# Sparse attention and a hardswish FFN as one pipeline over 384-token tiles, with head pairs on 128 partitions

## The chip, the cores and the metric

One core of a Trainium2 chip. The metric is the device time of one execution in microseconds (us). Engines: PE (matrix multiply; PEld its weight loads), DVE (vector), ACT (scalar), POOL (GpSimd), SP (issues DMA only). "Clock" is the share of full speed that the throttle granted the PE.

## The reference

Inputs q, k, v are (4 batches, 8 heads, 768 tokens, 64), float32. Cut to what matters:

```python
k_sum = k.reshape(B, H, 24, 32, D).max(axis=3)       # one summary per block of 32 keys
v_sum = v.reshape(B, H, 24, 32, D).mean(axis=3)
mask  = |i - j| < 16                                 # local window
scores = concat(where(mask, q k^T / 8, -1e9), q k_sum^T / 8 + log(32))
x = softmax(scores) @ concat(v, v_sum)               # to (3072 tokens, 512)
h = x @ w_in                                         # 512 -> 2048
out = (h * clip(h + 3, 0, 6) / 6) @ w_out            # 2048 -> 512
```

## The kernel before

A Tile scheduler orders its instructions. Heads go one by one; tokens sit in blocks of 128:

```python
for b in range(B):
    for h in range(H):
        ...  # qs, ks, vsf: float32 loads through SP, two buffers each
        for st in range(ST):                              # 6 blocks of 128 tokens
            tp = ps.tile([64, 128], F32, tag="scr")
            nc.tensor.transpose(tp[:], qs[:, st, :], ident[:])
            nc.vector.tensor_copy(qT[:, st * 128:(st + 1) * 128], tp[:])
            ...  # the same for ks; later six of v with reduce_sum
        for jt in range(ST):
            nc.tensor.matmul(sp[:, :w], klhs, qr, start=True, stop=True)     # up to 128 x 384
            nc.vector.tensor_scalar_mul(ap[:, :w], sp[:, :w], scl)
            nc.gpsimd.affine_select(out=ap[:, :w], ...)   # two of them: the band
            nc.scalar.activation(ap[:, :w], ap[:, :w], AF.Exp)
        ...
        for st in range(ST):
            ...  # up to 4 matmuls into op [128, 65], reciprocal, scale, transpose, copy
            nc.sync.dma_start(out=x4[b, h, :, st * 128:(st + 1) * 128], in_=oT[:])   # to a DRAM scratch
...
for tt in range(TT):                                      # 6 tiles of 512 tokens, x read back
    for ft in range(NFT):
        ...  # FFN1: 4 matmuls into hp [128, 512]
        nc.vector.tensor_scalar(hs[:], hp[:], 3.0, 0.0, op0=ALU.add, op1=ALU.max)
        nc.vector.tensor_scalar(gt, hs[:], 6.0, 1.0 / 6.0, op0=ALU.min, op1=ALU.mult)
        nc.vector.tensor_tensor(gt, gt, hp[:], op=ALU.mult)
    ...  # FFN2: per 128 tokens 16 matmuls into [128, 512], copy, store
```

The softmax here doesn't subtract the row's maximum and nothing guards it: scores larger than these inputs give would overflow.

Of the kernel before, what the change touches and what calls it, by code (L numbers as in the profile page):

```python
# [9 lines left out]
F32 = mybir.dt.float32  # L10
BF16 = mybir.dt.bfloat16
AF = mybir.ActivationFunctionType
ALU = mybir.AluOpType
AX = mybir.AxisListType


@with_exitstack
def kernel(
# [9 lines left out]
    nc = tc.nc  # L28
    B, H, S, D = q.shape
    block, window = 32, 16  # L30
    nb = S // block
    scl = 1.0 / math.sqrt(D)
    logb = math.log(block)
    NEG = -1.0e9
    ST = S // 128
    d_model = H * D
    n_tok = B * S
    d_ff = moe_w_in.shape[1]

    x_dram = nc.dram_tensor("x_scratch", (d_model, n_tok), BF16, kind="Internal").ap()  # L40
    x4 = x_dram.rearrange("(h d) (b s) -> b h d s", b=B, h=H)

    qv = q.rearrange("b h (st p) d -> b h p st d", p=128)
    kv = k.rearrange("b h (st p) d -> b h p st d", p=128)
    vv = v.rearrange("b h (st p) d -> b h p st d", p=128)

    sb = ctx.enter_context(tc.tile_pool(name="sb", bufs=2))
    ps = ctx.enter_context(tc.tile_pool(name="ps", bufs=2, space=bass.MemoryType.PSUM))
    const = ctx.enter_context(tc.tile_pool(name="const", bufs=1))

    ident = const.tile([128, 128], F32, tag="id")
    make_identity(nc, ident[:])
    identb = const.tile([128, 128], BF16, tag="idb")
    nc.vector.tensor_copy(identb[:], ident[:])
    ones = const.tile([128, 1], F32, tag="ones")
    nc.vector.memset(ones[:], 1.0)

    for b in range(B):
        for h in range(H):
            qs = sb.tile([128, ST, 64], F32, tag="qs")  # L60
            ks = sb.tile([128, ST, 64], F32, tag="ks")
            vsf = sb.tile([128, ST, 64], F32, tag="vsf")
            nc.sync.dma_start(out=qs[:], in_=qv[b, h])
            nc.sync.dma_start(out=ks[:], in_=kv[b, h])
            nc.sync.dma_start(out=vsf[:], in_=vv[b, h])
            vs = sb.tile([128, ST, 65], BF16, tag="vs")
            nc.vector.tensor_copy(vs[:, :, :64], vsf[:])
            nc.vector.memset(vs[:, :, 64:65], 1.0)
            qT = sb.tile([64, ST * 128], BF16, tag="qT")
            kT = sb.tile([64, ST * 128], BF16, tag="kT")  # L70
            for st in range(ST):
                tp = ps.tile([64, 128], F32, tag="scr")
                nc.tensor.transpose(tp[:], qs[:, st, :], ident[:])  # L73
                nc.vector.tensor_copy(qT[:, st * 128:(st + 1) * 128], tp[:])  # L74
                tp2 = ps.tile([64, 128], F32, tag="scr")
                nc.tensor.transpose(tp2[:], ks[:, st, :], ident[:])  # L76
                nc.vector.tensor_copy(kT[:, st * 128:(st + 1) * 128], tp2[:])  # L77
            ksT = sb.tile([64, nb], BF16, tag="ksT")
            nc.vector.reduce_max(ksT[:], kT[:].rearrange("d (n b) -> d n b", b=block), axis=AX.X)
            vsumT = sb.tile([64, nb], F32, tag="vsumT")  # L80
            for st in range(ST):
                tp = ps.tile([64, 128], F32, tag="scr")
                nc.tensor.transpose(tp[:], vsf[:, st, :], ident[:])  # L83
                nc.vector.reduce_sum(vsumT[:, st * 4:st * 4 + 4],  # L84
                                     tp[:].rearrange("d (n b) -> d n b", b=block), axis=AX.X)
            vsum = sb.tile([128, 65], BF16, tag="vsum")
            nc.vector.memset(vsum[:], 0.0)
            nc.vector.memset(vsum[:nb, 64:65], 1.0)  # L88
            vp = ps.tile([nb, 64], F32, tag="scr")
            nc.tensor.matmul(vp[:], vsumT[:], ident[:64, :64], start=True, stop=True)  # L90
            nc.vector.tensor_scalar_mul(vsum[:nb, :64], vp[:], 1.0 / block)

            ap_store = {}
            for jt in range(ST):
                st_lo = max(0, jt - 1)
                st_hi = min(ST, jt + 2)
                w = (st_hi - st_lo) * 128
                klhs = kT[:, jt * 128:(jt + 1) * 128]
                qr = qT[:, st_lo * 128:st_hi * 128]
                sp = ps.tile([128, 384], F32, tag="scr")  # L100
                nc.tensor.matmul(sp[:, :w], klhs, qr, start=True, stop=True)  # L101
                ap = sb.tile([128, 384], BF16, tag=f"ap{jt}")
                nc.vector.tensor_scalar_mul(ap[:, :w], sp[:, :w], scl)  # L103
                base = (jt - st_lo) * 128
                nc.gpsimd.affine_select(  # L105
                    out=ap[:, :w], in_=ap[:, :w], compare_op=ALU.is_ge, fill=NEG,
                    base=base + (window - 1), channel_multiplier=1, pattern=[[-1, w]])
                nc.gpsimd.affine_select(  # L108
                    out=ap[:, :w], in_=ap[:, :w], compare_op=ALU.is_ge, fill=NEG,
                    base=-base + (window - 1), channel_multiplier=-1, pattern=[[1, w]])  # L110
                nc.scalar.activation(ap[:, :w], ap[:, :w], AF.Exp)  # L111
                ap_store[jt] = (ap, st_lo)
            spA = sb.tile([nb, S], BF16, tag="spA")
            for half in range(2):
                sp = ps.tile([nb, 384], F32, tag="scr2")
                nc.tensor.matmul(sp[:], ksT[:], qT[:, half * 384:(half + 1) * 384],
                                 start=True, stop=True)
                nc.vector.tensor_scalar(spA[:, half * 384:(half + 1) * 384], sp[:], scl, logb,  # L118
                                        op0=ALU.mult, op1=ALU.add)
            nc.scalar.activation(spA[:], spA[:], AF.Exp)  # L120

            for st in range(ST):
                jts = [jt for jt in (st - 1, st, st + 1) if 0 <= jt < ST]
                nj = len(jts) + 1
                op = ps.tile([128, 65], F32, tag="op")
                for ii, jt in enumerate(jts):
                    ap, st_lo = ap_store[jt]
                    lhs = ap[:, (st - st_lo) * 128:(st - st_lo + 1) * 128]
                    nc.tensor.matmul(op[:], lhs, vs[:, jt, :], start=(ii == 0), stop=False)  # L129
                nc.tensor.matmul(op[:], spA[:, st * 128:(st + 1) * 128], vsum[:nb, :],  # L130
                                 start=False, stop=True)
                inv = sb.tile([128, 1], F32, tag="inv")
                nc.vector.reciprocal(inv[:], op[:, 64:65])
                o = sb.tile([128, 64], F32, tag="o")
                nc.vector.tensor_scalar_mul(o[:], op[:, :64], inv[:])  # L135
                otp = ps.tile([64, 128], F32, tag="scr")
                nc.tensor.transpose(otp[:], o[:], ident[:])  # L137
                oT = sb.tile([64, 128], BF16, tag="oT")
                nc.vector.tensor_copy(oT[:], otp[:])  # L139
                nc.sync.dma_start(out=x4[b, h, :, st * 128:(st + 1) * 128], in_=oT[:])  # L140

    KT = d_model // 128
    NFT = d_ff // 128
    MT = d_model // 128
    N_TOK_TILE = 512
    TT = n_tok // N_TOK_TILE

    wconst = ctx.enter_context(tc.tile_pool(name="wc", bufs=1))
    w_in_f = wconst.tile([128, KT, d_ff], F32, tag="winf")
    nc.sync.dma_start(out=w_in_f[:], in_=moe_w_in.rearrange("(kt p) f -> p kt f", p=128))  # L150
    w_out_f = wconst.tile([128, NFT, d_model], F32, tag="woutf")
    nc.sync.dma_start(out=w_out_f[:], in_=moe_w_out.rearrange("(ft p) dm -> p ft dm", p=128))
    w_in_sb = wconst.tile([128, KT, d_ff], BF16, tag="win")
    nc.vector.tensor_copy(w_in_sb[:], w_in_f[:])
    w_out_sb = wconst.tile([128, NFT, d_model], BF16, tag="wout")
    nc.vector.tensor_copy(w_out_sb[:], w_out_f[:])

    sb2 = ctx.enter_context(tc.tile_pool(name="sb2", bufs=2))
    ps2 = ctx.enter_context(tc.tile_pool(name="ps2", bufs=2, space=bass.MemoryType.PSUM))
    gpool = ctx.enter_context(tc.tile_pool(name="gp", bufs=1))  # L160

    xTv = x_dram.rearrange("(kt p) (tt t) -> tt kt p t", p=128, t=N_TOK_TILE)
    for tt in range(TT):
        xk = []
# [53 lines left out]
```

## Time and profile before

| | before |
|---|---|
| time, median of 5 runs | 826.98 us |
| PE, DVE, ACT, POOL busy | 74%, 72%, 14%, 21% |
| attention ends | 733 us |
| one head | about 21 us |
| mean clock in the record | 0.797 |

### The profile page before, as it was taken

The numbers are of one execution on the slowest core, as the hardware profiler recorded it, in microseconds if no ns is written. First come the engines' busy times: TensorE is split into PE (matmuls) and PEld (weight loads), VectorE is DVE, ScalarE is ACT, GpSimd is POOL, SyncE is SP. The second block draws the span as 40 slices with busy tenths as digits, with TensorE's granted clock in tenths as the row PEclk, the third lists the DMA queues.
The fourth block names the chain that finished last, engine by engine and source line by source line (L and its number), as shares of the span: only waits on it lengthen the run. The fifth ranks groups of instructions, "written<-read, shape, count | busy, mean of one in ns | idle before, by whom it ended". The sixth has DMA issues, their size and how long they took to land.

```text
span 825.3 us, 9346 instructions
## 1 busy us (share of the span) xinstructions
PE 610.6 (74%) x2560; PEld 259.3 (31%) x2560; DVE 596.2 (72%) x1916; ACT 116.7 (14%) x225; POOL 170.1 (21%) x390
## 2 busy tenths in 40 slices
PE   5167666767787967667779978797788967665857
PEld 1022222222333422223334433343334322222323
DVE  5476666667878766668887888877888766669493
ACT  1011111111111111111111111111111111110000
POOL 2022222221122222222210222222211222220000
PEclk9999999999957965556666985698667955558999
DMA  8711111111111221111111211121111211000101
GB/s 260 235 33 39 35 39 34 41 34 41 34 27 26 80 53 40 41 39 39 32 35 42 80 29 26 34 71 51 34 40 44 84 35 27 6 18 1 51 1 51
DMA packets 100180, 40.46 MB, mean 49 GB/s; under 512 B 91424, under 2 KB 94496, under 8 KB 99616
## 3 DMA queue, kind: packets, MB, share of 16 engines
q1 hardware_dynamic: 100128, 39.87, 18.1%
q8 instruction: 20, 0.33, 0.2%
q14 instruction: 32, 0.26, 0.1%
HBM read 30.41 MB, written 9.44 MB: 48 GB/s over the span
## 4 chain that ended last, share of the span: by engine, by line
issue 75%; POOL 13%; PE 6%; DVE 4%; POOLq 1%; DMA 0%; ACT 0%; SPq 0%
POOL ap L105 8%; POOL ap L108 6%; PE op L184 3%; PE hp L174 3%; DVE hs L176 2%; DVE g L179 1%; DVE g L178 1%; POOLq L105 0%; POOLq L108 0%; DMA xt<-x_scratch 0%; PE otp L137 0%; DVE oT L139 0%; PE op L129 0%; DVE ot L186 0%; PE op L130 0%
## 5 line engine op out<-in xcount | busy, mean ns | idle before, releaser
L105 POOL TENSOR_SCALAR_AFFINE_SELECT ap<-ap 128x384 bf16<-128x384 bf16 (+1 forms) x192 | 87.5, 471 | 555.5 <-DVE ap L103 555.3
L174 PE MATMUL hp<-xt,w_in_sb 128*128 128x512 bf16 x384 | 147.1, 486 | 34.2 <-DVE g L179 30.2
L73 PE MATMUL tp<-ident,qs 128*64 128x128 f32 x192 | 72.4, 377 | 55.4 <-DVE oT L139 44.7
L103 DVE TENSOR_SCALAR ap<-sp 128x384 bf16<-128x384 f32 (+1 forms) x192 | 95.9, 513 | 23.8 <-PE sp L101 19.5
L111 ACT ACTIVATE ap<-ap 128x384 bf16<-128x384 bf16 (+1 forms) x192 | 88.5, 484 | 120.9 <-POOL ap L108 120.0
L129 PE MATMUL op<-vs,ap 128*128 128x65 bf16 x512 | 82.2, 240 | 31.3 <-ACT ap L111 31.2
L184 PE MATMUL op<-w_out_sb,g 128*128 128x512 bf16 x384 | 102.4, 390 | 3.4 <-DVE g L179 3.4
L120 ACT ACTIVATE spA<-spA 24x768 bf16<-24x768 bf16 x32 | 26.9, 842 | 492.6 <-DVE spA L118 459.5
L108 POOL TENSOR_SCALAR_AFFINE_SELECT ap<-ap 128x384 bf16<-128x384 bf16 (+1 forms) x192 | 89.1, 480 | 4.4
L137 PE MATMUL otp<-ident,o 128*64 128x128 f32 x192 | 72.4, 398 | 23.4 <-DVE vsum L88 12.2
L129 PEld LDWEIGHTS <-ap 128*128 128x128 bf16 x512 | 59.5, 127 | 95.9 <-ACT ap L111 69.3
L139 DVE CAST oT<-otp 64x128 bf16<-64x128 f32 x192 | 52.2, 278 | 46.5 <-DMA x_scratch<-oT 30.3
L76 PE MATMUL tp<-ident,ks 128*64 128x128 f32 x192 | 72.0, 375 | 18.6 <-DVE kT L77 11.9
L101 PE MATMUL sp<-qT,kT 64*128 64x384 bf16 (+1 forms) x192 | 78.4, 412 | 10.0 <-DVE ap L103 3.6
L77 DVE CAST kT<-tp 64x128 bf16<-64x128 f32 x192 | 53.8, 280 | 35.5 <-PE tp L76 34.7
L176 DVE TENSOR_SCALAR hs<-hp 128x512 f32<-128x512 f32 x96 | 64.5, 674 | 8.3 <-PE hp L174 7.5
L74 DVE CAST qT<-tp 64x128 bf16<-64x128 f32 x192 | 53.7, 280 | 19.6 <-PE tp L73 19.4
L174 PEld LDWEIGHTS <-w_in_sb 128*128 128x128 bf16 x384 | 42.3, 113 | 74.9 <-issue 58.4
L83 PE MATMUL tp<-ident,vsf 128*64 128x128 f32 x192 | 57.3, 354 | 11.4 <-DVE vsumT L84 8.4
L179 DVE TENSOR_TENSOR g<-g,hp 128x512 bf16<-128x512 bf16 x96 | 64.6, 673 | 0.5
L135 DVE TENSOR_SCALAR o<-op,inv 128x64 f32<-128x64 f32 x192 | 53.0, 276 | 2.8
L73 PEld LDWEIGHTS tp<-ident,qs 128*64 128x64 f32 x192 | 25.4, 132 | 90.1 <-DVE oT L139 58.2
(33 smaller groups left out, 464.5 us busy)
## 6 DMA issues: line engine op xcount, KB each, us to landing
qs<-in_q_dram SPq DMA_DIRECT2D x32, 192.0 KB, 2.8
ks<-in_k_dram SPq DMA_DIRECT2D x32, 192.0 KB, 2.9
vsf<-in_v_dram SPq DMA_DIRECT2D x32, 192.0 KB, 2.5
out_dram<-ot SPq DMA_DIRECT2D x24, 256.0 KB, 2.0
w_in_f<-in_moe_w_in_dram SPq DMA_DIRECT2D x1, 4096.0 KB, 13.5
w_out_f<-in_moe_w_out_dram SPq DMA_DIRECT2D x1, 4096.0 KB, 15.5
x_scratch<-oT SPq DMA_DIRECT2D x192, 16.0 KB, 1.7
xt<-x_scratch SPq DMA_DIRECT2D x24, 128.0 KB, 2.2
```

Source lines behind the costliest of these rows:

```text
L73: nc.tensor.transpose(tp[:], qs[:, st, :], ident[:])
L101: nc.tensor.matmul(sp[:, :w], klhs, qr, start=True, stop=True)
L103: nc.vector.tensor_scalar_mul(ap[:, :w], sp[:, :w], scl)
L105: nc.gpsimd.affine_select(out=ap[:, :w], in_=ap[:, :w], compare_op=ALU.is_ge, fill=NEG, base=base + (window - 1), channel_multiplier=1, pa ...
L108: nc.gpsimd.affine_select(out=ap[:, :w], in_=ap[:, :w], compare_op=ALU.is_ge, fill=NEG, base=-base + (window - 1), channel_multiplier=-1, ...
L111: nc.scalar.activation(ap[:, :w], ap[:, :w], AF.Exp)
L129: nc.tensor.matmul(op[:], lhs, vs[:, jt, :], start=(ii == 0), stop=False)
L137: nc.tensor.transpose(otp[:], o[:], ident[:])
L174: nc.tensor.matmul(hp[:], lhs, xk[kt][:], start=(kt == 0), stop=(kt == KT - 1))
L176: nc.vector.tensor_scalar(hs[:], hp[:], 3.0, 0.0, op0=ALU.add, op1=ALU.max)
L179: nc.vector.tensor_tensor(gt, gt, hp[:], op=ALU.mult)
L184: nc.tensor.matmul(op2[:], lhs, w_out_sb[:, ft, :], start=(ft == 0), stop=(ft == NFT - 1))
```

## The change

Its intent: fewer, wider operations in attention, no DRAM scratch, and matmuls of three tiles mixed on a PE whose order the kernel now fixes itself. Two heads share 128 partitions, with k and v laid out block-diagonally. Keys go in blocks of 64, so a local score block is 64 keys of two heads by 94 queries. The core of the diff, cut:

```diff
+    ctx.enter_context(tc.manual_schedule(engines={ET.PE}))
...
+    def load_k(b, p):                       # casts to bf16 on the way; q and v likewise
+        nc.gpsimd.dma_start(out=t[:, :, j], in_=k[b, 2 * p + j]...)
...
+    def vsum(b, g):                         # sums of 32 rows by halving
+        eng = nc.vector if b == 0 else nc.gpsimd
...
+    def Tk(b, p):                           # k transposes: 6 into one PSUM tile
+        tp = ps_t.tile([128, S], BF16, tag="t", name="tk")         # ps_t: one buffer
+        nc.scalar.activation(t[0:64, :, 0:64], tp[0:64]..., AF.Copy)
+        nc.vector.tensor_copy(t[64:128, :, 64:128], tp[64:128]...)
+        nc.vector.reduce_max(red[:], tp[:]..., axis=AX.X)
+    def Tq(b, p, lo, hi):                   # q transposes: the same PSUM tile
+    def Sl(b, p, lo, hi):                   # local scores
+        nc.scalar.activation(a, sp[:, 0:n * WIN]..., AF.Exp, scale=scl)
+        eng = nc.vector if b == 0 else nc.gpsimd
+        eng.tensor_tensor(a, a, mask..., op=ALU.mult)
+    def AVn(b, p, half): ...                # numerators; AVd: denominators, Ln, Exp(-), multiply
...
+    def F1(t, ft):                          # 4 matmuls of 384 columns
+        nc.scalar.activation(r[:], hp[:], AF.Relu, bias=half_c[:], scale=1.0 / 6.0)
+        nc.vector.scalar_tensor_tensor(gt[t][:, ft], r[:], 1.0, hp[:], op0=ALU.min, op1=ALU.mult)
...
+    for stage in range(NTILE + 2):          # NTILE = 8; stage 0 is attention alone
+        for i in range(NFT):
+            F1(stage - 1, i)
+            F2(stage - 2, 3 * i .. 3 * i + 2)
+            ...  # then attention steps of tile `stage`, two per step in even stages, until step 13
```

An even stage also transposes k for its batch; an odd stage has the second half of the same batch.

## The prediction

> **What bounds the kernel now.** I read the page's totals and slices first, then the chain that ended last, then the costliest groups, then busy time by window.
>
> ```profile
> PE 610.6 (74%) x2560; PEld 259.3 (31%) x2560; DVE 596.2 (72%) x1916; ACT 116.7 (14%) x225; POOL 170.1 (21%) x390
> ...
> PEclk9999999999957965556666985698667955558999
> ...
> issue 75%; POOL 13%; PE 6%; DVE 4%; POOLq 1%; DMA 0%; ACT 0%; SPq 0%
> ...
> L174 PE MATMUL hp<-xt,w_in_sb 128*128 128x512 bf16 x384 | 147.1, 486 | 34.2 <-DVE g L179 30.2
> L73 PE MATMUL tp<-ident,qs 128*64 128x128 f32 x192 | 72.4, 377 | 55.4 <-DVE oT L139 44.7
> L184 PE MATMUL op<-w_out_sb,g 128*128 128x512 bf16 x384 | 102.4, 390 | 3.4 <-DVE g L179 3.4
> ```
>
> No engine is full: PE and DVE each about three quarters, and they wait for each other. The chain in order of time shows the rhythm:
>
> ```profile
> 60.02 15.78 issue
> 81.19 15.31 issue
> 101.89 16.57 issue
> ...
> 766.14 13.97 PE op L184 x64
> ```
>
> One head comes about every 21 us (60.02, 81.19, 101.89) and 32 heads end at 733 us. FFN tiles of finished batches fill gaps from about 195 us on; after 733 us the last FFN tiles stand alone for 92 us. So the bound is a latency loop in attention: a 128x128 transpose, a 280 ns copy out, the next, with two score buffers; then per block scale on DVE, two POOL selects, Exp. DVE work of attention is (596.2 minus 194.6 for FFN evacuation and weight casts)/32 = 12.5 us of each 21 us.
>
> The clock matters too. Busy time by window:
>
> ```profile
> core 0: us, PE busy (x) PEld busy (x) DVE busy (x) ACT busy (x) POOL busy (x), PEclk, DMA share, GB/s
> 0.00:60.00 60.00, 26.17 (x97) 10.18 (x98) 34.12 (x97) 7.94 (x14) 11.14 (x30) 1.00 0.57 181
> 60.00:200.00 140.00, 97.69 (x379) 39.58 (x378) 91.20 (x337) 22.05 (x44) 31.40 (x73) 1.00 0.16 37
> 200.00:733.00 533.00, 423.93 (x1833) 184.35 (x1833) 410.95 (x1377) 86.73 (x168) 127.53 (x288) 0.70 0.16 41
> 733.00:825.30 92.30, 62.79 (x252) 25.22 (x252) 59.88 (x108) 0.00 (x0) 0.00 (x0) 0.92 0.08 27
> ```
>
> The 1.00 of the first 200 us is not to be believed: the 128x384 score matmul has the same median record, 474 ns, from 100 to 120 us as from 300 to 320 us, where the clock reads 0.50. The PE runs attention at half speed and FFN at full speed. The 13.97 us for 64 second-FFN matmuls is 218 ns each at 512 columns: full rate.
>
> **What the Trainium skill says.** (1) "TensorE: Matmul & The Clock Gate", Back-to-back issue gap: N/2.4 + 2.5 ns warm, N/1.2 ns cold. This trace agrees: 218 ns against 216. (2) The same page, What's actually happening: the gate follows how busy the PE has been, with 1.2 and 2.4 GHz. The trace agrees: 0.50 in pure attention, 0.92 in the end phase, although PE is busy only 63 of 92 us there. (3) "GPSIMD Engine Reference", Elementwise side-by-side cycle accounting: a tensor_tensor of 2048 fp32 takes 4497 ns, 2.2 ns per element. No such POOL operation is in the trace before. (4) "DMA: Bandwidth & Descriptors", SWDGE vs HWDGE vs iDMA: a DMA that casts must be issued from GpSimd, where software writes the descriptors. Before, all DMA goes through SP (0.4 to 0.8 us per issue), so no run shows its cost.
>
> **The change part by part.**
>
> *Removed:* 576 float32 transposes of q, k, v (202 us of PE records), 192 of o and their copies, 384 POOL selects (176 us), the scale pass on DVE, the DRAM scratch and its reload, and the float32 weight staging with its wait for w_out (10.7 us). DVE loses two of three FFN1 passes (64.5 + 40.2 us): Relu goes to ACT, one fused min-multiply stays.
>
> *PE after, from the built program, at full clock.* FFN1: 512 matmuls of 384 columns x 162.5 ns = 83 us. FFN2: 384 x 218 ns = 84 us. Attention: 192 transposes x 56 = 11; 192 score blocks of 94 columns x 45 = 9 (65-column matmuls in a row start 35 ns apart warm and 65 ns cold in the trace, so weight loads hide); 32 summary scores x 162 = 5; numerators 32 x 162 + 224 short x about 40 = 14; denominators 64 x 162 + 64 short x 40 = 13. Sum 52 us, total 219 us.
>
> *ACT after:* 384 elements took 523 ns and 256 took 408 before. 128 Relu + 32 Ln + 32 Exp at 0.52 = 100; 24 output copies at 0.64 = 15; 16 k copies of 768 at 0.84 = 13; 48 score Exps at 0.41 to 0.60 = 25; 16 summaries = 8. Total 161 us.
>
> *DVE after:* a 384-element operation on PSUM is 673 - 128 x 1.03 = 541 ns, the slope from the 557 and 425 ns rows. 160 of them = 87; k copies, maxima and q copies 16 x (0.87 + 0.93 + 0.60 + 0.42) = 45; set-up memsets, first batch's masks and v sums about 35. Total 165 us. *POOL:* 36 masks of 376 x 2.2 ns = 30; six v sums of 2016 elements = 27; 104 DMA issues, which I choose at 1 us each = 104. Total 161 us.
>
> So PE becomes the busiest engine, but it is in program order, with one transpose buffer, one numerator, one denominator and one FFN2 output.
>
> *Stages.* PE work: stage 1 (FFN1 + attention) 16 us; stages 2, 4, 6 (FFN1 10.4 + FFN2 10.5 + attention with k transposes 7.6) 28.5 each; 3, 5, 7 26.3 each; stage 8 21; stage 9 10.5. Sum 212 us.
>
> *Stalls I add, by count.* In even stages three of four q transposes stand directly behind the k transposes of the same buffer and wait for a DVE copy and a maximum (0.87 + 0.93 + handover = 2 us): 6.5 us. At each of three FFN2 outputs per stage the next accumulation waits for the 0.64 us copy and the queue ahead: 3 us. The last numerators wait for Ln, Exp and multiply (about 1.6 us): 1.5 us. A rest of 1 us. That makes even stages 41, odd 32, stage 1 22, stage 8 24, stage 9 with its last store 14: 22 + 123 + 96 + 24 + 14 = 279 us.
>
> *Start.* Sixteen casting loads stand ahead of the identity on POOL (about 18 us); DVE has 32 zeroing memsets of about 0.45 us, four of about 2 us (1 element per ns from small memsets) and waits for the identity in between: first k copy at about 35 us. Then stage 0 alone, cold, with about 20 us of DVE work in a chain of latencies: 25 us. FFN1 starts near 60 us; 10.4 MB needed by then at the 240 GB/s of the old start are 43 us, hidden. Sum: 60 + 279 = 339; I say **335 us**.
>
> **The rivals.** (a) *POOL becomes the bound.* A casting load is 768 rows of 256 B; if it costs 3 us of POOL and not 1, a batch of two stages holds 24 x 3 + 21 = 93 us of POOL against 73 us of PE, the start grows by 30 us, and the time is about 430. For it: masks, v sums and loads share one in-order queue; against: SP issues the same shapes in 0.5 us. (b) *PE stays at half clock.* Then 430 us of PE alone, about 500. Against it: the old end phase kept 0.92 with PE busy two thirds. (c) *Stalls overlap fully*, PE dense: 212 + 55 = 267 plus a little, about 285. Against it: single buffers on an in-order PE. (d) *DMA bound:* still about 40 MB, 133 GB/s over 300 us against 303 GB/s reached in the old start; the rows are as short as before; hidden after the start.
>
> **Range and chances.** Stalls may be 30 us less or 40 more, the start 15 less or 30 more. Range **290 to 390**. Faster by over 2%: 0.99, since even (b) with the slow start is far below 826; same 0.005; slower 0.005.
>
> **What would show it.** PE about 70% of the span with the clock at 0.9 or more from stage 1; one 384-token tile finished every 30 to 41 us; first FFN1 matmul near 60 us; PE waits led by copies out of the transpose buffer, the output copy on ACT and the numerator multiply; ACT and DVE each near 50%. Wrong: POOL over 80%, masks or loads as leading releasers (rival a); clock under 0.8 in the middle (b); first FFN1 past 80 us (start mis-sized).

## The result, and the profile after

The changed kernel takes 374.82 us (median of 5, 373.65 to 378.27) against 826.98. The ratio is 0.4548, 95% interval 0.4526 to 0.457. Ratios are the mean time of one kernel's fast runs over that of the other's in the same rounds, so not quite the ratio of the medians.

The page of the changed kernel: busy time; five rows of the span in 40 slices (busy tenths, granted clock, DMA share, GB/s); the chain that ended last; four of the costliest groups.

```profile
PE 255.8 (68%) x1696; PEld 143.2 (38%) x1696; DVE 158.8 (42%) x336; ACT 157.2 (42%) x297; POOL 152.5 (41%) x203
...
PE   0000257886670179898857798989477989899985
...
POOL 8992102899999933276334032520020302200000
PEclk9999999999798559999978899999788999999999
DMA  9999999997997660197763001900000000001011
GB/s 76 92 107 191 187 183 203 146 136 109 133 145 69 42 42 30 34 106 72 70 40 25 28 30 31 89 28 17 13 0 30 29 29 29 28 14 43 30 56 56
...
PE 54%; POOL 16%; ACT 10%; DMA 9%; DVE 6%; issue 4%; POOLq 0%; ACTq 0%
...
L348 PE MATMUL op<-wout,g 128*128 128x512 bf16 x384 | 110.8, 399 | 13.9 <-ACT ot L352 13.7
L334 PE MATMUL hp<-x,win 128*128 128x384 bf16 x512 | 115.3, 351 | 1.6 <-DVE g L338 0.8
L338 DVE SCALAR_TENSOR_TENSOR g<-r,hp 128x384 bf16<-128x384 f32 x128 | 70.7, 553 | 103.6 <-ACT r L337 103.0
L337 ACT ACTIVATE r<-hp,half_c 128x384 f32<-128x384 f32 x128 | 73.8, 577 | 85.4 <-PE hp L334 83.5
```

The FFN now heads the list and its matmuls lead the chain. But POOL, only 41% busy, holds 16% of the chain, and its row is solid nines from slice 8 to 13. Just there PE drops to "0 1" in slices 12 and 13 and the clock to 5 (slices 13 and 14). Who waited for whom shows it as well (us in total, times, longest):

```profile
PE tq L216 <- DVE red L205: 53.2, 16, 17.7
PE num L260 <- POOL at L230: 16.3, 2, 16.2
PE tk L200 <- DVE ident L118: 15.8, 1, 15.8
PE op L348 <- ACT ot L352: 13.7, 17, 0.9
POOL kb L84 <- DMA win<-in_moe_w_in_dram: 12.4, 2, 6.9
```

Three single waits are long. Two of them, 17.7 and 15.8 us, lie in stage 0, before 35 us; the one of 16.2 us is the only long one after it. The stages come from the PE timeline, each counted from its first FFN1 matmul (FFN2 for the last):

| stage | predicted us | measured us |
|---|---|---|
| 0 (set-up, attention alone) | 60 | 65.9 |
| 1 | 22 | 24.8 |
| 2 | 41 | **64.8** |
| 3, 5, 7 | 32 each | 30.3 each |
| 4, 6 | 41 each | 45.5, 45.1 |
| 8, 9 | 24, 14 | 23.8, 15.8 |
| sum | 339 | 376.5 |

So 24 of the 37 us that the sum missed lie in stage 2. (The profiled execution was the slowest of the five, 378.27 us or 3.5 us over the median. Differences of stages between profiles carry some us of that.) The next fence is busy time by window for stages 2, 3 and 4: the busy time of PE, its weight loads and the three other engines, then clock, DMA share and GB/s.

```profile
core 0: us, PE busy (x) PEld busy (x) DVE busy (x) ACT busy (x) POOL busy (x), PEclk, DMA share, GB/s
90.70:155.50 64.80, 37.46 (x233) 20.43 (x233) 22.77 (x36) 20.91 (x40) 47.06 (x57) 0.76 0.77 72
155.50:185.70 30.20, 26.98 (x193) 15.18 (x192) 11.66 (x24) 17.51 (x34) 18.51 (x24) 1.00 0.89 79
185.70:231.30 45.60, 34.56 (x234) 19.37 (x233) 19.09 (x36) 21.57 (x42) 11.00 (x14) 0.89 0.25 31
```

Stage 2 holds the same PE, DVE and ACT work as stage 4, within two instructions. What differs is POOL, 47 us in place of 11, and the DMA share, 0.77 in place of 0.25. PE in stage 2 (start, duration, operation, count, idle before and its releaser):

```profile
90.66 0.81 PE L334 MATMUL hp<-x,win 128*128 128x384 bf16 x4 [0.59 <-DVE g L338]
...
91.96 0.50 PE L200 MATMUL tk<-ident,kb 128*128 128x128 bf16 x6
95.01 0.58 PE L216 MATMUL tq<-ident,qb 128*128 128x128 bf16 x4 [2.55 <-DVE red L205]
95.39 1.48 PE L334 MATMUL hp<-x,win 128*128 128x384 bf16 x4
...
113.48 0.33 PE L257 MATMUL num<-asum,vst 128*128 128x384 bf16 x1
129.98 0.46 PE L260 MATMUL num<-at,vbd 128*128 128x79 bf16 x4 [16.17 <-POOL at L230]
```

and POOL in the same stretch:

```profile
110.64 2.38 POOL L183 TENSOR_TENSOR va<-vf 128x1024 f32<-128x1024 f32 x1
...
120.19 2.34 POOL L183 TENSOR_TENSOR va<-vf 128x1024 f32<-128x1024 f32 x1
...
123.81 1.73 POOL L84 DMA_DIRECT2D kb<-in_k_dram  x2
...
129.07 1.48 POOL L230 TENSOR_TENSOR at<-at,mask 128x376 bf16<-128x376 bf16 x2
```

POOL never idles; it is late. It works through the v sums of batches 2 and 3 and through loads before the first mask of batch 1, which the PE needs at 113.8 us, comes at 129.1. The first PE lines show a second, smaller loss. Four FFN1 matmuls take 0.81 us at the start of the stage, and 1.48 us after the k transposes and a wait of 2.55 us. (The record of the last one adds its own latency; starts are 0.16 and 0.32 us apart, which is full and half speed.) Stage 4 begins in the same way: 0.81 us at 185.74, 1.49 us at 190.63.

### The profile page after: what moved, and what is told of

Its sections match the earlier page's. It is cut to its first block, busy times and chain, and to the rows that moved or that the text cites. A ratio compares the mean times of both kernels' runs of the same rounds, so it can differ in the third digit from the quotient of the medians.

```text
span 376.5 us, 4613 instructions
## 1 busy us (share of the span) xinstructions
PE 255.8 (68%) x1696; PEld 143.2 (38%) x1696; DVE 158.8 (42%) x336; ACT 157.2 (42%) x297; POOL 152.5 (41%) x203
## 4 chain that ended last, share of the span: by engine, by line
PE 54%; POOL 16%; ACT 10%; DMA 9%; DVE 6%; issue 4%; POOLq 0%; ACTq 0%
PE hp L334 21%; PE op L348 20%; DMA wout<-in_moe_w_out_dram 9%; POOL vbd L96 3%; POOL va L186 3%; ACT ot L352 3%; POOL qb L90 3%; POOL kb L84 3%; POOL va L183 2%; DVE red L205 2%; PE num L260 2%; PE num L257 2%; ACT kbd L202 2%; PE sl L225 2%; PE tq L216 2%
## 5 line engine op out<-in xcount | busy, mean ns | idle before, releaser
L348 PE MATMUL op<-wout,g 128*128 128x512 bf16 x384 | 110.8, 399 | 13.9 <-ACT ot L352 13.7
L334 PE MATMUL hp<-x,win 128*128 128x384 bf16 x512 | 115.3, 351 | 1.6 <-DVE g L338 0.8
L338 DVE SCALAR_TENSOR_TENSOR g<-r,hp 128x384 bf16<-128x384 f32 x128 | 70.7, 553 | 103.6 <-ACT r L337 103.0
L337 ACT ACTIVATE r<-hp,half_c 128x384 f32<-128x384 f32 x128 | 73.8, 577 | 85.4 <-PE hp L334 83.5
L230 POOL TENSOR_TENSOR at<-at,mask 128x376 bf16<-128x376 bf16 (+2 forms) x36 | 30.2, 843 | 105.7 <-ACT at L228 105.7
L334 PEld LDWEIGHTS <-win 128*128 128x128 bf16 x512 | 48.5, 104 | 30.5 <-issue 8.2
L348 PEld LDWEIGHTS <-g 128*128 128x128 bf16 x384 | 39.4, 103 | 49.2 <-issue 20.1
L216 PE MATMUL tq<-ident,qb 128*128 128x128 bf16 x96 | 12.8, 255 | 55.1 <-DVE red L205 53.2
L90 POOL DMA_DIRECT2D qb<-in_q_dram x32 | 27.0, 864 | 31.7 <-PE tq L216 19.5
L84 POOL DMA_DIRECT2D kb<-in_k_dram x32 | 27.2, 867 | 27.5 <-DMA win<-in_moe_w_in_dram 12.4
L202 ACT ACTIVATE kbd<-tk 64x768 bf16<-64x768 bf16 x16 | 12.8, 802 | 43.9 <-PE tk L200 43.5
L260 PE MATMUL num<-at,vbd 128*128 128x94 bf16 (+2 forms) x224 | 15.1, 210 | 16.3 <-POOL at L230 16.3
L96 POOL DMA_DIRECT2D vbd<-in_v_dram x32 | 24.6, 781 | 3.7 <-DMA wout<-in_moe_w_out_dram 3.5
L200 PE MATMUL tk<-ident,kb 128*128 128x128 bf16 x96 | 10.0, 254 | 20.1 <-DVE ident L118 15.8
L352 ACT ACTIVATE ot<-op 128x512 f32<-128x512 f32 x24 | 14.2, 592 | 11.6 <-PE op L348 11.2
## 6 DMA issues: line engine op xcount, KB each, us to landing
win<-in_moe_w_in_dram POOLq DMA_DIRECT2D x4, 512.0 KB, 21.3
wout<-in_moe_w_out_dram POOLq DMA_DIRECT2D x4, 512.0 KB, 35.1
```

Of the source, the lines that this page charges most:

```text
L84: nc.gpsimd.dma_start(out=t[:, :, j], in_=k[b, 2 * p + j].rearrange("(s p) d -> p s d", p=128))
L90: nc.gpsimd.dma_start(out=t[:, :, j], in_=q[b, 2 * p + j].rearrange("(s p) d -> p s d", p=128))
L96: nc.gpsimd.dma_start(out=t[j * 64:(j + 1) * 64, :, j * 64:(j + 1) * 64], in_=v[b, 2 * p + j].rearrange("(n p) d -> p n d", p=KB))
L216: nc.tensor.transpose(tp[:, (st - lo) * 128:(st - lo + 1) * 128], src[:, st], ident[:])
L230: eng.tensor_tensor(a, a, mask[:].unsqueeze(1).to_broadcast([128, n, WIN]), op=ALU.mult)
L260: nc.tensor.matmul(num[:, lo:hi], vbd[e][p][:, t], at[e][p][:, t, off:off + hi - lo], start=False, stop=(i == len(bl) - 1))
```

## The experiments

Twelve kernels, 4 runs each (the profiled one and three rounds), all with correct results. All runs were fast but one of mask_dve (364.32 us, slow); the ratios use fast runs alone. Times are medians; before was 824.8 to 826.4 us in these sessions. The last three two_t runs and packed were taken in a later session and on another chip than vsum_two_t, so differences of about 1 us between them are not shown.

| label | edit on the changed kernel | us | ratio to before |
|---|---|---|---|
| vsum_dve | v sums on DVE | 358.56 | 0.4354 |
| mask_dve | masks on DVE | 358.46 | 0.4343 |
| weights_sp | weights through SP, cast on ACT | 368.28 | 0.4463 |
| spread | k and q transposes in different FFN steps | 352.28 | 0.4272 |
| vsum_spread | both | 337.17 | 0.4079 |
| vsum_two_t | v sums on DVE, two transpose buffers | 330.49 | 0.4004 |
| two_t_f2 | vsum_two_t and FFN2 groups at step starts | 322.06 | 0.3900 |
| two_t_start | vsum_two_t and zeroing on ACT | 329.73 | 0.3994 |
| two_t_both | both of these | **319.48** | 0.3870 |
| unfused | v sums on DVE, no overlap of attention and FFN | 440.47 | 0.5336 |
| *on the kernel before:* ffn_only | FFN1 epilogue only | 795.21 | 0.9627 |
| packed | packed transposes only | 761.85 | 0.9241 |

### Why stage 2 is long: three ways to relieve POOL

```diff
 # vsum_dve
-        eng = nc.vector if b == 0 else nc.gpsimd     # in vsum
+        eng = nc.vector
 # mask_dve
-        eng = nc.vector if b == 0 else nc.gpsimd     # in Sl
+        eng = nc.vector
 # weights_sp (w_in shown, w_out alike)
-        nc.gpsimd.dma_start(out=w_in_sb[...], in_=w_in_v[...])
+        wf = gp.tile([128, NP, w], F32, tag="g", name="wf")
+        nc.sync.dma_start(out=wf[:], in_=w_in_v[...])
+        nc.scalar.activation(w_in_sb[...], wf[:], AF.Copy)
```

> Edit: the v sums of batches 1 to 3 go from POOL to DVE, nothing else. Theory A (stage 2 is 65 us against 41 for stages 4 and 6 because POOL, in order, still works through loads and v sums when the first mask of batch 1 is due): about 36 us of POOL work leave, the 16.2 us wait of the numerators for the mask falls under 3 us, stage 2 falls to 42 to 48 us, the span to 350 to 358 us. Rival B (stage 2 is long because the weights and the batch 1 data land late): stage 2 stays over 58 us, the span at 368 to 376 us. Rival C (DVE gets too full): the chunk of 20 us of v sums delays the PE by over 5 us in later stages.

> Edit: the masking of the local probabilities goes to DVE for all batches (0.30 to 0.51 us each there against 0.68 to 1.01 us on POOL), the v sums stay on POOL. Theory A: POOL leaves the path to the numerators, the 16.2 us wait goes, span 348 to 358 us, unless the batch 1 v sums on POOL (done at 90 us) are themselves late. Rival B: stage 2 over 58 us, span 368 to 376 us.

> Edit: both weights are loaded as float32 through SP into the two idle g buffers and cast on ACT, in place of eight casting loads on POOL. Theory A2 (POOL fell behind because its load queue was held from 30 to 68 us by the slow casting weight loads): the prefetch of batch 1 goes out about 30 us earlier, POOL reaches the masks in time, the 16.2 us wait goes although the v sums stay on POOL, stage 2 is 42 to 48 us, span 345 to 360 us. Rival A1 (the v sums ahead of the masks are enough by themselves): a wait of over 8 us stays, span over 362 us. The start (first FFN1 matmul at 65.9 us) may move either way by 8 us.

With the v sums moved, the wait for the mask is gone from the list of PE waits, stage 2 takes 44.9 us and the total falls by 16.3 us. With the masks moved it falls by 16.4 us, stage 2 takes 47.1. Both totals are about the 16.2 us of the one wait and end 0.5 us above the range expected: theory A holds, and DVE was not too full (its longest list of v sums cost no later stage more than noise). Rival B falls for this wait.

weights_sp leaves all v sums on POOL and still brings the mask wait to 0.3 us and stage 2 to 48.9 us. So the backlog has two parents: the v sums that stand ahead of the masks, and POOL's own lateness from the start. In the changed kernel POOL issues eight loads between 30 and 68 us and stands still otherwise, and the trace puts most of these issues down to the weight loads (the 12.4 us line above, and as much again for q). Removing either parent is enough for the mask wait. The total gained 6.5 us only and ended at 368.3 us, where rival A1 had it (over 362), because the start got longer: first FFN1 at 74.0 us and not 65.9. Beside the big SP loads POOL waited for earlier k and q loads before it could issue the next (1.8 and 3.7 us, no such wait in the changed kernel), and the identity behind them came late (the first transpose waited 21.9 us for it, 15.8 before).

### The short waits: the transpose buffer

```diff
 # spread: in even stages from 2 on, steps listed by FFN step i
+   order = [[Tk0], [Tq0], [Tk1], [Tq1, v0, Sl0a], [Tk2, Sl0b], [Tq2, Sl1a], [Tk3, Sl1b, Ss0], [Tq3, AVn0], ...]
 # vsum_two_t: on top of vsum_dve, order as in the change
-   ps_t bufs=1; ps_s bufs=2
+   ps_t bufs=2; ps_s bufs=1
```

> Edit: in even stages from 2 on, the k transposes and the q transposes of a head pair stand in different FFN steps, so FFN matmuls fill the wait for the one transpose buffer. Theory D (the 2.55 us waits for the maximum are lost PE time and let the clock fall): 3 stages x 3 waits x 1.3 us or more come back, span 355 to 365 us, stages 4 and 6 at 36 to 39 us each. Rival E (the waits were shadow of ACT and DVE work that must be done anyway): stages 4 and 6 stay at 41 us, span 370 to 377 us.

> Edit: both the v sums on DVE and the spread transposes. Theory (two separate losses that add: the POOL backlog of 16 us, which grew to 24.9 us under the spread order, and the transpose-buffer waits): 374.8 - 16 - 22.5 - 8.7 more of unhidden backlog = 328 us, so 324 to 334 us. Rival (DVE work placed on the v sums delays the k copies and takes some back): 336 to 345 us.

> Edit: on top of the v sums on DVE (358.6 us), the order of the changed kernel is kept but the transpose gets two PSUM buffers and the scores one. Theory D (the loss is the single transpose buffer, not the order): the 53 us of waits of the q transposes for the maximum fall under 10 us, also in stage 0; span 330 to 342 us. Rival (the waits move: one score buffer holds the PE, or the PE then waits for q copies and Exp instead): span 345 to 360 us.

spread gained 22.5 us, more than expected: stages 4 and 6 fell from 45 to 35.5 us each. It did so although it made the other loss worse:

```profile
PE tq L216 <- DVE red L205: 36.4, 13, 17.7
PE num L260 <- POOL at L230: 24.9, 2, 23.1
```

The PE reached the first numerators sooner and waited 23.1 us for the same late mask. In stage 4 the q waits fell from 8.9 to 3.3 us, and the same 233 matmuls took 29.5 us of PE time in place of 34.5, at a clock of 1.00 in place of 0.89. So about half of the 10 us is the waits and half is the clock that no longer falls behind them. Rival E falls.

Both edits together gave 337.2 us where adding up had said 328: above the range of the sum and at the lower edge of the rival's. Stage 2 stayed at 44.0 us, with 4.6 us of mask waits and POOL at 32 us of work; so the lateness of POOL was not wholly gone.

Two transpose buffers did more than the new order: 330.5 us, within the range of theory D. Stages 4 and 6 take 33.2 us, and stage 0 shortens by 8 us, where spread did not act. The waits of q transposes for the maximum fell from 53.2 to 2.2 us; one wait of 17.2 us for it, now before a k transpose, stays in stage 0. The price was small: waits of the scores for their single buffer are 2.9 us, of the summaries 7.6 us. But stage 2 still takes 50.6 us, now for another reason:

```profile
PE tq L216 <- DMA qb<-in_q_dram: 9.7, 2, 9.5
PE tk L200 <- DMA kb<-in_k_dram: 3.9, 1, 3.9
```

The loads of batch 1 themselves land late, since POOL could not issue them before the weight loads were through. That is rival B of the first experiment, but the move of the v sums made it worse. POOL's last wait for w_out ended at 67.5 us in the changed kernel, at 79.5 in vsum_dve and at 86.6 here. With its sums on DVE, a v-sum tile comes free earlier, and SP issued its sixteen v loads (384 KB each) by 77 us and not by 109: all of them now run beside the weight loads, and not the first eight alone. That these loads are what slows the weights is read from the traces; no run held them back.

### The small rest, and the start

```diff
 # two_t_f2
-                for j in range(3):
-                    F2(f2, 3 * i + j)
+                for j in range(F2_AT[i], F2_AT[i + 1]):     # a new output group starts at step 0, 6 and 12
+                    F2(f2, j)
 # two_t_start
-        nc.vector.memset(vfull[g][32:64], 0.0)              # and the second batch's off-diagonal zeros
+        nc.scalar.activation(dst, zero..., AF.Copy)         # on ACT, idle then
```

> Edit: on top of v sums on DVE and two transpose buffers (330.5 us), FFN2 starts each 128-row output group at the start of an FFN step, behind four FFN1 matmuls, and no longer in the middle of a step. Theory: 13.7 us of PE waits for the output copy (17 waits) fall under 4 us, span 318 to 324 us. Rival (the PE then waits for FFN1 evacuation instead): 326 to 332 us.

> Edit: on top of v sums on DVE and two transpose buffers, the zeroing of the v-sum tiles and of the second batch's block-diagonal tiles goes from DVE to ACT, which is idle in the first 30 us. Theory S (DVE set-up work holds the first k copy at 32.5 us): first FFN1 matmul moves from 57.1 to 44 to 50 us, span 317 to 325 us. Rival T (the slow casting loads set the start: the loads of batch 0 or the first weights land no earlier): first FFN1 at 54 to 60 us, span 327 to 334 us.

> Both edits of the two runs before. If they act in different stretches they add: 306 to 318 us.

two_t_f2 gained 8.4 us, as expected: the waits for the output copy fell from 13.7 to 2.1 us. two_t_start gained under 1 us, which is not a shown difference: the 95% intervals of its ratio and of vsum_two_t's overlap. The first FFN1 came at 53.0 us in place of 57.1, not at 44 to 50: taking the zeroing off DVE did not help much, because something else came late. POOL and PE of that run:

```profile
18.25 0.82 POOL L90 DMA_DIRECT2D qb<-in_q_dram  x1 [2.55 <-DMA qb<-in_q_dram]
21.29 0.82 POOL L90 DMA_DIRECT2D qb<-in_q_dram  x1 [2.23 <-DMA qb<-in_q_dram]
...
22.61 0.30 POOL masks.py:199 TENSOR_SCALAR_AFFINE_SELECT identf<-identf 128x128 f32<-128x128 f32 x1
```

The tile for the v sums is loaded as soon as it is zeroed, so its loads now ran beside the casting k and q loads. POOL waited for earlier loads before it could issue those (2.55 and 2.23 us above), and the identity matrix, which stands behind them in POOL's order, came at 22.6 us and not at 15.0. The first transpose waited 23.3 us for it. Of the 4 us gained there the profile shows 1.7 lost again in stage 2 (52.3 us), where the mask wait came back with 12.3 us, and 0.4 in the last stage. Rival T, that the casting loads set the start, is nearer the truth than theory S. two_t_both, at 319.5 us, is 11 us under vsum_two_t, a little outside its expected range; it is the fastest kernel. Its stage 2 still takes 52 us against 32 for stages 4 and 6, with 11.6 us in one mask wait. What a better issue of the first loads would give was not tried, nor was fixing the order of POOL's instructions by hand, as the change does for PE.

### What the 450 us are made of

```diff
 # unfused: per batch, on top of vsum_dve
+        attention of both tiles;  F1(2b);  F1(2b + 1) with F2(2b);  F2(2b + 1)
 # ffn_only: the kernel before, FFN1 epilogue of the change
-            three DVE operations
+            nc.scalar.activation(hs[:], hp[:], AF.Relu, bias=half_c[:], scale=1.0 / 6.0)
+            nc.vector.scalar_tensor_tensor(g[:, ft, :], hs[:], 1.0, hp[:], op0=ALU.min, op1=ALU.mult)
 # packed: the kernel before
-            per 128 tokens: tp [64, 128], transpose, copy
+            for lo, hi in ((0, 4), (4, ST)):     # tp [64, 512], 4 or 2 transposes, one copy or one reduce_sum
```

> Edit: with the v sums on DVE, the pipeline is undone: per batch both attention tiles alone, then FFN1 and FFN2 of both tiles alone, same operations on the same engines. Theory F (most of the gain over the kernel before comes from the cheaper attention, the rest from the overlap and the clock): attention alone about 30 us for an even tile and 20 for an odd, 4 x 50 = 200, FFN 4 x 51 = 204, start 32: 420 to 450 us, the clock in attention 0.50. Rival G (the overlap is most of the gain): over 560 us. Rival H (the PE order hides little): under 390 us.

> Edit: the kernel before with only the FFN1 epilogue changed (Relu with bias on ACT, one fused min-multiply on DVE in place of three DVE passes). Theory: 105 us of DVE work leave; after 733 us the two FFN1 loops are paced at 1.73 us a block by 1.79 us of DVE and fall to about 1.05 us, 32 blocks give 22 us; before that the freed DVE time shortens attention, which waits on DVE latency and not on DVE throughput, by 10 to 50 us: 750 to 800 us. Rival (DVE throughput is the bound in the mixed part): under 730 us.

> Edit: the kernel before, with only the transposes of q, k and v of a head packed four and two to a PSUM bank and copied or summed out in one operation each: 18 handovers of PE and DVE per head become 6; no transpose is removed, none is cheaper. Theory P (attention is bound by the number of handovers): the stretch of q and k transposes of 5.5 us per head falls to about 3.3 us and v saves up to 1 us, 32 x 2.2 to 3.2 us = 70 to 100 us, so 725 to 755 us. Rival Q (the float32 transposes at half clock are the cost): under 30 us gained, over 795 us.

unfused takes 440.5 us, as theory F said. The windows are one batch of attention, one batch of FFN, and attention again (columns as before):

```profile
131.00:182.50 51.50, 27.98 (x212) 18.61 (x211) 14.84 (x31) 17.50 (x36) 28.45 (x36) 0.58 0.68 48
182.50:234.00 51.50, 43.88 (x220) 21.36 (x218) 18.29 (x33) 22.14 (x39) 0.74 (x1) 0.99 0.13 30
234.00:284.50 50.50, 27.45 (x209) 18.30 (x208) 13.41 (x27) 18.18 (x37) 19.84 (x24) 0.61 0.39 30
```

Eight heads of attention take 51 us by themselves, where the kernel before took about 168 (8 x 21). That is the larger part of the gain: unfused against before is 384 us. (unfused also has the cheaper FFN1 epilogue and no DRAM scratch, and the kernel before already hid most FFN tiles in attention, so the 384 us are not attention's alone.) The overlap is worth 440.5 - 358.6 = 82 us. Part of that is the clock: attention alone is granted 0.58 to 0.61, beside FFN it ran at 0.89 and above from stage 3 on.

What made attention cheap? packed changes nothing in it but the number of handovers, with the copies made wider, and gains 64.6 us: between the two expectations and near theory P. Wider copies also saved DVE 50 us of busy time (546.4 against 596.2); the run does not part the two. The stretch of q and k transposes of one head in packed:

```profile
100.55 1.06 PE L75 MATMUL tp<-ident,qs 128*64 128x128 f32 x4 [1.44 <-DVE oT L139]
101.41 1.06 PE L75 MATMUL tp<-ident,ks 128*64 128x128 f32 x4
102.39 0.64 PE L75 MATMUL tp<-ident,qs 128*64 128x128 f32 x2
103.24 0.64 PE L75 MATMUL tp<-ident,ks 128*64 128x128 f32 x2 [0.22 <-DVE kT L76]
103.67 1.49 PE L83 MATMUL tp<-ident,vsf 128*64 128x128 f32 x6
```

It lasts 3.1 us, from 100.55 to the first v transpose; before it took 5.0 us (714.72 to 719.74 us; 5.0 and 5.5 by turns for the heads near 100 us). The q and k part came out as expected; v added nothing that shows in the total. Where the PE and DVE hand a small tile back and forth, packing alone is worth 2 us a head. The other parts of the cheaper attention (pairs, masks after Exp, normalising on wide tiles) were not tried one by one.

ffn_only gained 29.7 us, within its range. In the last FFN1 loop, two blocks take 2.52 us in place of 3.46.

The clock record of packed settles a doubt as well:

```profile
PEclk9985555555777596556766897766987778969999
```

Its attention reads 5 from slice 3 on, where the kernel before reads 9 for the first 200 us with the same matmul durations. The PE was at half speed there too.

## Why the prediction was right or wrong

The time was within the range, 40 us above the point. By its steps:

- **What bounds the kernel before** (a loop of handovers at half clock): right. packed shortens the loop without cheaper transposes, and reads the clock of 0.5 that the first record hid.
- **The engine sums**: right in their totals, in part because errors offset. ACT 161 against 157.2 us, DVE 165 (its terms add up to 167) against 158.8, POOL 161 against 152.5. On POOL the masks were right (30.2 us); a casting load costs 0.78 to 0.87 us where I chose 1, so the issues took 85 and not 104 us; but the six v sums took 37 us and not 27, since one has 2240 elements and not 2016 and costs more per element than 2.2 ns (2397 ns for 1024). FFN1 groups start 0.65 us apart warm: four of 162.5 ns, as reckoned. DVE copies out of the bf16 PSUM tile are cheaper than I took (561 and not 870 ns for k), and Relu is dearer (577 and not 523 ns).
- **The start**: 60 against 65.9 us. The first k copy came at 32.5 us, expected 35; the attention of stage 0 behind it took 33 us, not 25.
- **Stages 1 and 3 to 9**: within 5 us each. Stage 1 was 3 us higher, stages 3, 5 and 7 were 2 us lower. The even ones were 4 us higher: their q waits are 8.9 us where the prediction has 6.5, and the matmuls behind them run at half clock, 5.0 us a stage by the comparison with spread, which it left out.
- **Stage 2, the step that failed.** The prediction gave it the same 41 us as stages 4 and 6: it added up POOL's work for the whole kernel, but not when that work could be done. The rate was not the error. The page of the profile counts a casting load at its bf16 size (96 KB for 768 rows of 256 B), so the 143 GB/s of the first 60 us are, by an estimate that counts the casting queue's bytes twice (5.4 of 8.6 MB), about 230 GB/s of float32 read, close to the 240 of the prediction. What it missed is that all eight weight loads, w_out too, stand in one queue ahead of batch 1, and that POOL waits for them: it was not free of these waits until 68 us, and it met the first mask of batch 1 with v sums and loads undone. Measured: 64.8 us, of which 16.2 are one wait; the three relief experiments show the cause.
- **The rivals.** (a) was wrong in its number (0.87 us per load, not 3; POOL 41% busy) but named the engine: it was late once and not full. (b) and (d) fell as said: the clock reads 0.89 to 1.00 from stage 3 on, and the DMA row is near empty from slice 26 on. (The mean of 0.93 is too high: the record reads 1.00 in stage 1, where four FFN1 matmuls at 69.06 us take 1.48 us. And DMA was not idle at first: its row reads 9 for the first twelve slices.) (c) is what the edits move towards: 319.5 us, not 285.
- **Output copies**: 13.7 us measured, where 3 us a stage had been put in for about eight stages.

## What to carry to other kernels

A pipeline needs every in-order queue to be early, not only lightly loaded: an engine at 41% stopped the PE for 16 us because loads and sums of later batches stood ahead of the one mask that was due. When one wait is removed, look at the same stretch for the next wait beneath it, as stage 2 showed twice; and ask what the faster engine now starts earlier, as the v loads seem to have done to the weights. And count handovers before you count work: packing transposes gave 65 us without removing a single transpose, and a second PSUM buffer where two operations alternate gave 28.

## What the Trainium skill lacked or had wrong

- "DMA: Bandwidth & Descriptors", Measured, has a 1 MB load at 6.15 us and does not say whether it casts. No page that I read gives the rate of casting loads. Here eight of them, each 1 MiB of float32 cast to bf16, were issued together on POOL beside v loads from SP; POOL's waits for w_in ended at 37.2, 43.5, 50.4 and 57.4 us, 6.3 to 7.0 us apart. (The 21.3 and 35.1 us that the page of the profile gives from issue to landing are mostly time in the queue.)
- No page that I read says that POOL stands still before it can issue the next load while earlier casting loads are under way: 6.9 us at the longest in the changed kernel, 11.1 us in weights_sp.
